# Attention operands in two and a half loads, asked for a pair and two steps ahead, with a second buffer for the turned outputs

## Chip, cores and metric

One core of one Trainium2 chip runs the whole program. The metric is the device time of one execution in microseconds (us): the median of 3 runs before the change is 695.21 us (695.05 to 695.46).

## What is computed

Three layers in a row, in float32. Attention over 2 batches, 8 heads, 768 tokens and a head width of 64, where a query sees only the keys of its own cluster; then a mixing layer over the tokens and a feed-forward layer; then a gated feed-forward layer with a convolution of width 3.

```python
mask = q_assign[:, :, :, None] == k_assign[:, :, None, :]
scores = scale * np.matmul(q, k.transpose(0, 1, 3, 2))
scores = np.where(mask, scores, -1000000000.0)
scores = scores - np.max(scores, axis=-1, keepdims=True)
attn = np.exp(scores)
attn = attn / (np.sum(attn, axis=-1, keepdims=True) + 1e-09)
return np.matmul(attn, v).astype(np.float32)
...
h = xt @ U @ V
u = x + h.transpose(0, 2, 1)
ch = np.maximum(u @ w_ch1, 0.0) @ w_ch2
...
return (h * gate @ w_out).astype(np.float32)
```

`q_assign` and `k_assign` are the indices of the nearest of 16 centroids by cosine.

## The kernel before

**Tiles and steps.** The attention part walks over 96 query tiles of 128 rows: 2 batches, 4 pairs of heads, 2 heads, 6 tiles. One call of `step(n)` handles one tile with work of several tiles in flight: the scores of tile n+2 on TensorE (L342, L353), the exponentials of tile n+1 on ScalarE (L371), the transposes of tile n (L380), the split of tile n-1 into a rounded part (L389, ScalarE) and a rest (L393, VectorE), and one third of the product with the values for an earlier group of three tiles (L404). `s` is the step inside a pair of heads, 0 to 11; the pairs are numbered 0 to 7. The order of instructions on each engine is the order in which the program is written.

**Operands in two parts.** A float32 product is made from rounded (fp32r) parts: high times high, plus high times low, plus low times high. For each head there are two tiles. `cd` (80 partitions) holds the high parts of q and k in its first 64 partitions and one-hot cluster rows in the next 16, so that one matmul gives the high product and the mask. `ab` (128 partitions) holds low parts over high parts, for the two mixed products in one matmul. `load_ops` (L108) fills both by loads on the queue of POOL (GpSimd), which round to fp32r on the way: `ab[0:64]`, `ab[64:128]` and `cd[0:64]`, each 64 rows of q and k (384 KB). `split_ops` (L124) then makes the low parts on POOL, in two subtractions of 64x768: the unrounded q or k (`raw`, loaded through SP by `load_raw`, L89) less the rounded part that the load left in that same place of `ab`.

**Buffers.** Pools `ab` and `cd` have 3 buffers, one per head, so the load of a head reuses what the head three before it left. `raw` has 2, the values `vt` (L120) 2, their unrounded copy `rv` 1.

**Where the preparation stands.** `prep(n)` (L610) prepares the next pair while the present one runs: at s = 0 `load_raw` and the loads of its first head, at s = 2 that head's split, at s = 3 the loads of the values, at s = 4 the loads of the second head, at s = 5 its split, at s = 8 the low part of the values (L633, POOL), at s = 5 or 6 the one-hot rows (L265, SP). The first pair is prepared ahead of the loop (L526 to L532).

**What else is on POOL's queue.** Every third step (s = 1, 4, 7, 10) a group of three tiles ends. `step` then adds 1e-9 to the group's row sums on POOL (L681), and `fin_x` (L423) handles the group before: ScalarE copies the turned outputs out of PSUM into `ats` (L426), VectorE takes the reciprocal of that group's sums (L429), POOL adds the two halves of `ats` (L430) and scales them into `X` in three instructions (L434). `ats` has one buffer: the copy of a group waits until POOL has scaled the group before. ScalarE, VectorE and POOL each work through their queue in order, so a wait at the head of one holds up all behind it.

Of the kernel before, what the change touches and what calls it, by code (L numbers as in the profile page):

```python
# [15 lines left out]
F32 = mybir.dt.float32  # L16
# [8 lines left out]
P = 128  # L25
# [6 lines left out]
def tile_kernel(ctx: ExitStack, tc: tile.TileContext, qk, vv, cen, u_w, v_w, w1, w2, win, wout, conv, out):  # L32
    nc = tc.nc
    B, H, D, _, S = qk.shape
    NC = cen.shape[0] // H
    NP = H // 2
# [31 lines left out]
    a_e = att.enter_context(tc.tile_pool(name="a_e", bufs=3))  # L68
# [16 lines left out]
    raw = {}  # L85
    ops = {}
    vts = {}

    def load_raw(b, p, parts=1):  # L89
        rq, rk = raw[b, p] if (b, p) in raw else take_raw(b, p)  # L90
        h0 = 2 * p
        for i in range(parts):
            c = slice(i * S // parts, (i + 1) * S // parts)
            nc.sync.dma_start(out=rq[:, c], in_=qk[b, h0:h0 + 2, :, 0, c].rearrange("h d s -> (h d) s"))
            nc.sync.dma_start(out=rk[D:2 * D, c], in_=qk[b, h0, :, 1, c])
            nc.sync.dma_start(out=rk[0:D, c], in_=qk[b, h0 + 1, :, 1, c])

    def take_raw(b, p):
        raw[b, p] = tuple(a_raw.tile([P, S], F32, tag=t, name=t) for t in ("rq", "rk"))
        return raw[b, p]  # L100

    def take_ops(b, p, j):
        ab = a_ab.tile([P, 2, S], F32R, tag="ab", name="ab")
        cd = a_ab.tile([80, 2, S], F32R, tag="cd", name="cd")
        ops[b, 2 * p + j] = (ab, cd)
        return ab, cd

    def load_ops(b, p, j):  # L108
        h = 2 * p + j
        ab, cd = take_ops(b, p, j)  # L110
        nc.gpsimd.dma_start(out=ab[0:D], in_=qk[b, h])
        nc.gpsimd.dma_start(out=ab[D:2 * D], in_=qk[b, h])
        nc.gpsimd.dma_start(out=cd[0:D], in_=qk[b, h])

    def load_v(b, p):
        rv = a_v.tile([P, 2, NT, D], F32, tag="rv", name="rv", bufs=1)
        vt = a_v.tile([P, 2, NT, 2 * D], F32R, tag="vt", name="vt")
        nc.sync.dma_start(out=rv, in_=vv[b, p])
        for j in range(2):
            nc.gpsimd.dma_start(out=vt[:, j, :, 0:D], in_=vv[b, p, :, j])  # L120
        vts[b, p] = vt
        return rv, vt

    def split_ops(b, p, j, eng):  # L124
        rq, rk = raw[b, p]
        ab, _ = ops[b, 2 * p + j]
        q0, k0 = (0, D) if j == 0 else (D, 0)
        for r, i, p0 in ((rq, 0, q0), (rk, 1, k0)):
            eng.tensor_sub(ab[p0:p0 + D, i], r[p0:p0 + D], ab[p0:p0 + D, i])


    cent = acon.tile([P, 1, D], F32, name="cent")
# [60 lines left out]
    def split_first(half, which):  # L193
        c = slice(half * HS, (half + 1) * HS)
        if which == "k":
            nc.scalar.copy(cd0[0:D, 1, c], rk0[D:2 * D, c])
            nc.scalar.copy(ab0[0:D, 1, c], rk0[D:2 * D, c])
            nc.gpsimd.tensor_copy(ab0[D:2 * D, 1, c], rk0[D:2 * D, c])
            nc.vector.tensor_sub(ab0[D:2 * D, 1, c], rk0[D:2 * D, c], ab0[D:2 * D, 1, c])
        else:  # L200
            nc.scalar.copy(cd0[0:D, 0, c], rq0[0:D, c])
            nc.scalar.copy(ab0[D:2 * D, 0, c], rq0[0:D, c])
            nc.gpsimd.tensor_sub(ab0[0:D, 0, c], rq0[0:D, c], cd0[0:D, 0, c])
# [7 lines left out]
    def sims(b, p, tiles=range(NT)):  # L211
        rq, rk = raw[b, p]
        if (b, p) not in ohst:
            ohst[b, p] = {"pm": ps_t.tile([P, NT * 4, NC], F32, tag="t", name="sim")}
        pm = ohst[b, p]["pm"]
        for t in tiles:
            for i, (r, cb) in enumerate(((rq, cbq), (rk, cbk))):
                nc.tensor.matmul(
                    pm[:, 4 * t + 2 * i:4 * t + 2 * i + 2, :].rearrange("p g c -> p (g c)"),
                    r[:, t * P:(t + 1) * P], cb[:, p], start=True, stop=True,  # L220
                )

    def sims_onehot(b, p, part):

        v = ohst[b, p]
        if part == 0:
            v["mx"] = a_oh.tile([P, NT * 4, 1], F32, tag="mx", name="mx")
            v["eq"] = a_oh.tile([P, NT * 4, NC], BF16, tag="eq", name="eq")
            v["m2"] = a_oh.tile([P, NT * 4, 1], BF16, tag="m2", name="m2")
            v["oh"] = a_oh.tile([P, NT * 4, NC], BF16, tag="oh", name="oh")  # L230
        onehot_part(v, v["pm"], slice(0, NT * 4), part)
# [15 lines left out]
    def onehot_t(b, p):  # L247
        oh = ohst[b, p]["oh"]
        pt = ps_t.tile([4 * NC, S], BF16, tag="t", name="oht")
        for t in range(NT):  # L250
            nc.tensor.transpose(pt[:, t * P:(t + 1) * P], oh[:, 4 * t:4 * t + 4].rearrange("p g c -> p (g c)"), identb)
        ohst[b, p]["pt"] = pt

    def onehot_rows(b, p):
        pt = ohst.pop((b, p))["pt"]
        os_ = a_oh.tile([4 * NC, S], F32R, tag="os", name="os")
        nc.scalar.activation(os_, pt, AF.Identity, scale=ohs[:, 0:1], bias=ohs[:, 1:2])
        put_rows(b, p, os_, range(2))

    def put_rows(b, p, os_, heads):  # L260
        for j in heads:
            cd = ops[b, 2 * p + j][1]
            for i in range(2):
                r0 = (2 * i + j) * NC
                nc.sync.dma_start(out=cd[D:D + NC, i].bitcast(F32), in_=os_[r0:r0 + NC].bitcast(F32))  # L265
# [65 lines left out]
    def head_of(n):  # L331
        b, r = divmod(n, H * NT)
        h, t = divmod(r, NT)
        return b, h, t
# [87 lines left out]

    def fin_x(g):  # L423
        b, h, t0 = head_of(3 * g)
        at = a_e.tile([P, 3, 2, D], F32, tag="ats", name="ats", bufs=1)
        nc.scalar.copy(at, st.pop(("at", g)))  # L426
        sm = st.pop(("sum", g))
        rs = a_s.tile([P, 3, 1], F32, tag="rs", name="rs")
        nc.vector.reciprocal(rs[:, :, 0], sm)  # L429
        nc.gpsimd.tensor_add(at[:, :, 0], at[:, :, 0], at[:, :, 1])  # L430
        if h == 0 and t0 == 0:
            X[b] = xp.tile([P, NT, DM], F32, tag="x", name="x")
        for i in range(3):
            nc.gpsimd.tensor_tensor(  # L434
                out=X[b][:, t0 + i, h * D:(h + 1) * D], in0=at[:, i, 0],
                in1=rs[:, i].to_broadcast([P, D]), op=ALU.mult,
            )
# [48 lines left out]
    def pump(plan):  # L486

        for j in list(fly):
            j["at"] += 1
            if j["at"] in j["plan"]:  # L490
                j["plan"][j["at"]](j)
            if j["at"] == max(j["plan"]):
                fly.remove(j)
        if plan is THIN:
            free = not fly
        else:
            free = not fly or (fly[-1]["at"] > 1 and fly[-1]["plan"] is FLOW)
        if jobs and free:
            j = jobs.pop(0)
            j["at"], j["plan"] = 0, plan  # L500
            job_dma(j)
            fly.append(j)
# [21 lines left out]


    load_ops(0, 0, 1)  # L526
    rv0 = load_v(0, 0)
    first_pair()
    split_first(1, "q")
    sims(0, 1, range(2))  # L530
    split_ops(0, 0, 1, nc.gpsimd)
    nc.gpsimd.tensor_sub(rv0[1][:, :, :, D:2 * D], rv0[0], rv0[1][:, :, :, 0:D])  # L532

# [76 lines left out]
    def prep(n):  # L610

        pair, s = divmod(n, 2 * NT)
        nxt = pair + 1
        if nxt < B * NP:
            b, p = divmod(nxt, NP)
            for part, at in enumerate((2, 2, 3, 4, 5) if nxt > 1 else (0, 0, 1, 2, 3)):
                if s == at and (nxt > 1 or part > 1):
                    sims_onehot(b, p, part)
            if s == 0:
                if nxt > 1:  # L620
                    load_raw(b, p)
                load_ops(b, p, 0)
            elif s == 2:
                split_ops(b, p, 0, nc.gpsimd)
            elif s == 3:
                st["rv"] = load_v(b, p)
            elif s == 4:
                load_ops(b, p, 1)
            elif s == 5:
                split_ops(b, p, 1, nc.gpsimd)  # L630
            elif s == 8:
                rv, vt = st.pop("rv")
                nc.gpsimd.tensor_sub(vt[:, :, :, D:2 * D], rv, vt[:, :, :, 0:D])  # L633
            if s == (6 if nxt > 1 else 5):
                onehot_t(b, p)
                onehot_rows(b, p)
        if n == NQ - 7:
            queue_chunk(1, lambda: wpc)
        if n >= NQ - 7:
            pump(FLOW)  # L640
        elif n % 2 == 0 and n > 0:
            pump(THIN)

    def step(n):
# [39 lines left out]
        if 0 <= g - 1 < NHALF and r == 0:  # L684
            fin_x(g - 1)
# [194 lines left out]
    for i in range(len(order) + 2):  # L880
# [7 lines left out]
        if 0 <= i - 2:  # L888
            b, f = order[i - 2]
# [57 lines left out]
```

## Time and profile before

| what | value |
|---|---|
| median of 3 runs | 695.21 us |
| profiled execution | 694.12 us, span 692.2 us |
| TensorE (PE) busy | 666.3 us, 96% of the span |
| VectorE (DVE) busy | 445.8 us, 64% |
| ScalarE (ACT) busy | 373.0 us, 54% |
| GpSimd (POOL) busy | 298.9 us, 43% |
| DMA | 61.58 MB, mean 89 GB/s |
| granted TensorE clock, mean | 0.992 |

The span runs from the first to the last instruction of the profiled execution, and that execution's own time is 1.9 us longer. All profile times below are microseconds from the span's start. The attention part lasts to about 290 us. A busy share is a mean over stages, so it doesn't say by itself what a change in one stage is worth; the waits of that stage do.

### The profile page before, as it was taken

The page shows a single profiled execution, that of the slowest core. Times are in us where ns is not written, and L with a number is a line of the kernel's source. Part 1 is how long each engine was busy: PE and PEld are TensorE (multiplying, and loading weights), DVE is VectorE, ACT ScalarE, POOL GpSimd, SP SyncE. Part 2 cuts the span into 40 slices and gives each one's busy share as a digit, 9 for nine tenths or more (in the row PEclk, how much of TensorE's full clock was granted, in tenths as well). Part 3 has the DMA queues.
Part 4 walks back from the last instruction along what each step waited for, and adds up shares of the span by engine and source line. Part 5 has one row for each costly group of instructions (what it writes and reads, how often), then busy time and mean ns, then how long its engine had stood idle before and what let it go on. Part 6 is the DMA issues. An engine that isn't in the chain of part 4 may idle for free.

```text
span 692.2 us, 10474 instructions
## 1 busy us (share of the span) xinstructions
PE 666.3 (96%) x3782; PEld 586.0 (85%) x3782; DVE 445.8 (64%) x833; ACT 373.0 (54%) x750; POOL 298.9 (43%) x392
## 2 busy tenths in 40 slices
PE   8949999999999999999999999999999999999997
PEld 6849999999898998888888888888887788888886
DVE  6837888797978798749831778775237645643400
ACT  6837888787777898424311333433133457653611
POOL 6647666676666642515621333332015634332300
PEclk9988999999999999999999999999999999999999
DMA  9895768685666610301210333442003000000111
GB/s 195 151 136 115 165 116 197 108 192 103 167 119 153 131 35 5 118 31 63 92 62 1 121 123 121 142 133 92 1 30 125 28 0 1 1 32 16 43 49 46
DMA packets 32131, 61.58 MB, mean 89 GB/s; under 512 B 15856, under 2 KB 19568, under 8 KB 32080
## 3 DMA queue, kind: packets, MB, share of 16 engines
q1 hardware_dynamic: 15936, 40.08, 19.6%
q0 software_dynamic: 16144, 20.84, 17.6%
q8 instruction: 30, 0.49, 0.3%
q14 instruction: 21, 0.17, 0.1%
HBM read 56.29 MB, written 3.15 MB: 86 GB/s over the span
## 4 chain that ended last, share of the span: by engine, by line
PE 78%; DVE 8%; issue 3%; DMA 3%; ACT 3%; POOL 2%; ACTq 0%; POOLq 0%; DVEq 0%
PE g L836 10%; PE tr L380 7%; PE pv L404 7%; PE h L713 5%; PE h L715 5%; PE h L714 5%; PE a L730 5%; PE a L729 5%; PE a L731 5%; PE sc L342 3%; PE sc L353 3%; PE po L870 3%; PE po L871 3%; PE po L872 3%; DMA ab<-in_qk_dram 3%
## 5 line engine op out<-in xcount | busy, mean ns | idle before, releaser
L518 POOL TENSOR_TENSOR wl<-wx,wh 128x512 fp32r<-128x512 f32 x48 | 63.0, 1314 | 114.8 <-ACT wh L517 114.5
L393 DVE TENSOR_TENSOR pl<-tr,ph 128x384 fp32r<-128x384 f32 x192 | 97.6, 549 | 21.5 <-ACT ph L389 20.3
L380 PE MATMUL tr<-identf,e 128*128 128x128 f32 x576 | 83.7, 278 | 16.5 <-ACT ats L426 11.4
L389 ACT CAST ph<-tr 128x384 fp32r<-128x384 f32 x192 | 83.5, 485 | 21.3 <-PE tr L380 20.5
L359 DVE TENSOR_SCALAR_CACHE_REDUCE e<-sc 128x768 f32<-128x768 f32 x96 | 90.8, 947 | 0.6 <-PE sc L353 0.6
L718 ACT ACTIVATE rh<-h 128x512 fp32r<-128x512 f32 (+1 forms) x52 | 29.3, 563 | 111.7 <-PE h L715 111.7
L371 ACT ACTIVATE e<-sc,nb 128x768 f32<-128x768 f32 x96 | 88.4, 921 | 1.0 <-DVE e L359 0.9
L380 PEld LDWEIGHTS tr<-identf,e 128*128 128x128 f32 x576 | 66.9, 142 | 25.9 <-ACT ats L426 12.6
L719 DVE SCALAR_TENSOR_TENSOR rl<-h,rh 128x512 fp32r<-128x512 f32 (+1 forms) x52 | 33.7, 648 | 82.9 <-ACT rh L718 82.8
L713 PE MATMUL h<-uh,wh 128*128 128x512 f32 (+1 forms) x208 | 78.1, 376 | 1.6 <-DVE rl L719 1.6
L729 PE MATMUL a<-rh,wh 128*128 128x512 f32 (+1 forms) x208 | 78.1, 376 | 0.5 <-DVE xa L745 0.5
L730 PE MATMUL a<-rl,wh 128*128 128x512 f32 (+1 forms) x208 | 77.8, 374 | 0.5 <-DVE rl L719 0.3
L731 PE MATMUL a<-rh,wl 128*128 128x512 f32 (+1 forms) x208 | 77.6, 373 | 0.0
L715 PE MATMUL h<-uh,wl 128*128 128x512 f32 (+1 forms) x208 | 77.6, 373 | 0.0
L714 PE MATMUL h<-ul,wh 128*128 128x512 f32 (+1 forms) x208 | 77.6, 373 | 0.0
L404 PE MATMUL pv<-ph,vt 128*128 128x384 f32 x192 | 66.0, 344 | 0.2 <-ACT asb L413 0.2
L404 PE MATMUL pv<-pl,vt 128*128 128x384 f32 x192 | 65.3, 340 | 0.0
L517 ACT CAST wh<-wx 128x512 fp32r<-128x512 f32 x48 | 29.8, 620 | 58.3 <-DVE wx L471 58.1
L342 PE MATMUL sc<-ab 128*128 128x384 f32 x192 | 57.4, 381 | 0.7 <-ACT e L371 0.4
L853 POOL TENSOR_TENSOR h<-h,cv 128x768 f32<-128x768 f32 x16 | 29.6, 1850 | 64.5 <-ACT cv L852 64.5
L467 DVE SCALAR_TENSOR_TENSOR wx<-wb,wx 128x512 int32<-128x512 int32 (+3 forms) x52 | 48.3, 928 | 11.4 <-ACT wb L458 9.4
L353 PE MATMUL sc<-cd 80*128 80x384 f32 x192 | 49.7, 341 | 0.0
(136 smaller groups left out, 1493.4 us busy)
## 6 DMA issues: line engine op xcount, KB each, us to landing
raw<-in_w_dram SPq DMA_DIRECT2D x32, 512.0 KB, 3.7
ab<-in_qk_dram POOLq DMA_DIRECT2D x30, 384.0 KB, 5.2
cd<-in_qk_dram POOLq DMA_DIRECT2D x15, 384.0 KB, 6.8
raw<-in_win_dram SPq DMA_DIRECT2D x8, 512.0 KB, 3.7
raw<-in_wout_dram SPq DMA_DIRECT2D x8, 512.0 KB, 3.7
rv<-in_vv_dram SPq DMA_DIRECT2D x8, 384.0 KB, 3.4
vt<-in_vv_dram POOLq DMA_DIRECT2D x16, 192.0 KB, 3.6
out_dram<-o SPq DMA_DIRECT2D x24, 128.0 KB, 1.8
```

The lines of the kernel that those rows point to most:

```text
L359: nc.vector.tensor_scalar(out=e, in0=ps[:, :, 0:HS], scalar1=-SCALE, scalar2=3e38, op0=ALU.mult, op1=ALU.min, accum_out=nb,)
L371: nc.scalar.activation(e, ps[:, :, 0:HS], AF.Exp, scale=SCALE, bias=nb, accum_out=st["sum", n // 3][:, n % 3:n % 3 + 1])
L380: nc.tensor.transpose(pt[:, k, :], e[:, i, k * P:(k + 1) * P], identf)
L389: nc.scalar.copy(st["pt", n // 3][0][:, i * NK:(i + 1) * NK, n % 3, :], st["t", n, i])
L393: nc.vector.tensor_sub(lo, st.pop(("t", n, i)), hi)
L404: nc.tensor.matmul(acc, vt[:, h % 2, k, :], m[:, k].rearrange("p a b -> p (a b)"), start=(k == 0 and i == 0), stop=(k == NT - 1 and i == 1),)
L713: nc.tensor.matmul(ph, wh[:, k, ws], uh[g][:, k, ts], start=(k == 0), stop=False)
L714: nc.tensor.matmul(ph, wh[:, k, ws], ul[g][:, k, ts], start=False, stop=False)
L715: nc.tensor.matmul(ph, wl[:, k, ws], uh[g][:, k, ts], start=False, stop=(k == ND - 1))
L729: nc.tensor.matmul(accs[d][:, 0:n], wh[:, i, ds_], rh, start=(f == 0), stop=False)
L730: nc.tensor.matmul(accs[d][:, 0:n], wh[:, i, ds_], rl, start=False, stop=False)
L731: nc.tensor.matmul(accs[d][:, 0:n], wl[:, i, ds_], rh, start=False, stop=(f == NH - 1))
```

## The change

Each head's operands are loaded as `cd[0:64]` (q and k, 384 KB), `ab[64:128]` (q and k, 384 KB) and only the half of `ab[0:64]` that is used as it lands (192 KB). The other half of `ab[0:64]` is computed from `raw` and the rounded values in `cd`, which are the same numbers. In time, the loads of a pair's first head (and `load_raw`) are asked for at s = 10, two steps before the pair ahead of it begins; the first split follows at s = 1, the second head's loads at s = 3, the values' loads at s = 4, the second split at s = 7. For pair 1 the first head's loads stand in the code ahead of the loop. `ats` gets a second buffer.

```diff
@@ load_ops
-        nc.gpsimd.dma_start(out=ab[0:D], in_=qk[b, h])
+        nc.gpsimd.dma_start(out=cd[0:D], in_=qk[b, h])
         nc.gpsimd.dma_start(out=ab[D:2 * D], in_=qk[b, h])
-        nc.gpsimd.dma_start(out=cd[0:D], in_=qk[b, h])
+        nc.gpsimd.dma_start(out=ab[0:D, 1 - j], in_=qk[b, h, :, 1 - j])
@@ split_ops
-        rq, rk = raw[b, p]
-        ab, _ = ops[b, 2 * p + j]
-        q0, k0 = (0, D) if j == 0 else (D, 0)
-        for r, i, p0 in ((rq, 0, q0), (rk, 1, k0)):
-            eng.tensor_sub(ab[p0:p0 + D, i], r[p0:p0 + D], ab[p0:p0 + D, i])
+
+        ab, cd = ops[b, 2 * p + j]
+        lo, hi = raw[b, p][j], raw[b, p][1 - j]
+        eng.tensor_sub(ab[0:D, j], lo[0:D], cd[0:D, j])
+        eng.tensor_sub(ab[D:2 * D, 1 - j], hi[D:2 * D], ab[D:2 * D, 1 - j])
@@ fin_x
-        at = a_e.tile([P, 3, 2, D], F32, tag="ats", name="ats", bufs=1)
+        at = a_e.tile([P, 3, 2, D], F32, tag="ats", name="ats", bufs=2)
@@ ahead of the loop
     split_first(1, "q")
+    load_ops(0, 1, 0)
     sims(0, 1, range(2))
@@ prep
-            if s == 0:
-                if nxt > 1:
-                    load_raw(b, p)
-                load_ops(b, p, 0)
-            elif s == 2:
+            if s == 1:
                 split_ops(b, p, 0, nc.gpsimd)
             elif s == 3:
+                load_ops(b, p, 1)
+            elif s == 4:
                 st["rv"] = load_v(b, p)
-            elif s == 4:
-                load_ops(b, p, 1)
-            elif s == 5:
+            elif s == 7:
                 split_ops(b, p, 1, nc.gpsimd)
@@ prep, after the one-hot rows
+        if s == 10 and pair + 2 < B * NP:
+            load_raw(*divmod(pair + 2, NP))
+            load_ops(*divmod(pair + 2, NP), 0)
```

The instructions of TensorE, VectorE, ScalarE and SP keep their order; POOL's change. First place: POOL's queue around the start of pair 0, before. `ab_209` and `vt_215` are pair 0's second head and values, `ab_338` with `cd_339` is pair 1's first head.

```order
L120 DMA vt_215<-in_vv_dram 128x6x64 x2
L203 TENSOR_TENSOR ab_196<-rq_111,cd_197 64x384
L129 TENSOR_TENSOR ab_209<-rq_111,ab_209 64x768
L129 TENSOR_TENSOR ab_209<-rk_112,ab_209 64x768
L532 TENSOR_TENSOR vt_215<-rv_214,vt_215 128x12x64
L111 DMA ab_338<-in_qk_dram 64x1536
L112 DMA ab_338<-in_qk_dram 64x1536
L113 DMA cd_339<-in_qk_dram 64x1536
```

The same place now, where pair 1's first head is `ab_282` with `cd_283`.

```order
L120 DMA vt_215<-in_vv_dram 128x6x64 x2
L203 TENSOR_TENSOR ab_196<-rq_111,cd_197 64x384
L111 DMA cd_283<-in_qk_dram 64x1536
L112 DMA ab_282<-in_qk_dram 64x1536
L113 DMA ab_282<-in_qk_dram 64x768
L128 TENSOR_TENSOR ab_209<-rk_112,cd_210 64x768
L129 TENSOR_TENSOR ab_209<-rq_111,ab_209 64x768
L533 TENSOR_TENSOR vt_215<-rv_214,vt_215 128x12x64
```

Pair 1's first loads now stand ahead of the two splits of pair 0 and ahead of its values.

Second place: POOL's queue over the later steps of pair 0, before. `ab_450` with `cd_451` is pair 1's second head, `vt_417` its values; `sum_384` and `sum_476` are the row sums of the second and third group, `ats_558` and `x_563` belong to the first.

```order
L111 DMA ab_450<-in_qk_dram 64x1536
L112 DMA ab_450<-in_qk_dram 64x1536
L113 DMA cd_451<-in_qk_dram 64x1536
L129 TENSOR_TENSOR ab_450<-rq_180,ab_450 64x768
L129 TENSOR_TENSOR ab_450<-rk_181,ab_450 64x768
L681 TENSOR_SCALAR sum_384<-sum_384 128x3
L430 TENSOR_TENSOR ats_558<-ats_558 128x3x64
L434 TENSOR_TENSOR x_563<-ats_558,rs_560 128x64 x3
L633 TENSOR_TENSOR vt_417<-rv_416,vt_417 128x12x64
L681 TENSOR_SCALAR sum_476<-sum_476 128x3
```

The same place now: the second head is `ab_416` with `cd_417`, the values are `vt_451`, the first and second groups' sums are `sum_307` and `sum_386`, the first group's outputs `ats_556` and `x_561`.

```order
L111 DMA cd_417<-in_qk_dram 64x1536
L112 DMA ab_416<-in_qk_dram 64x1536
L113 DMA ab_416<-in_qk_dram 64x768
L681 TENSOR_SCALAR sum_307<-sum_307 128x3
L120 DMA vt_451<-in_vv_dram 128x6x64 x2
L681 TENSOR_SCALAR sum_386<-sum_386 128x3
L430 TENSOR_TENSOR ats_556<-ats_556 128x3x64
L434 TENSOR_TENSOR x_561<-ats_556,rs_558 128x64 x3
L128 TENSOR_TENSOR ab_416<-rk_181,cd_417 64x768
L129 TENSOR_TENSOR ab_416<-rq_180,ab_416 64x768
L630 TENSOR_TENSOR vt_451<-rv_450,vt_451 128x12x64
L681 TENSOR_SCALAR sum_476<-sum_476 128x3
```

Between the second head's loads and its split there is now the whole end of the first group, the second group's sums and the issue of the values' loads; before, the split followed its loads directly.

## Rows read from the trace of the kernel before

**Rows 1.** Page: busy us of each engine; PE's busy tenths in 40 slices

```profile
PE 666.3 (96%) x3782; PEld 586.0 (85%) x3782; DVE 445.8 (64%) x833; ACT 373.0 (54%) x750; POOL 298.9 (43%) x392
...
PE   8949999999999999999999999999999999999997
```

**Rows 2.** Waits, 15 to 275 us, all engines: us in total, times, longest

```profile
POOL ab L129 <- DMA ab<-in_qk_dram: 36.3, 8, 9.1
...
ACT ats L426 <- POOL x L434: 11.1, 1, 11.1
PE tr L380 <- ACT ats L426: 10.7, 3, 9.4
...
DVE rs L429 <- POOL sum L681: 9.2, 2, 8.9
...
ACT ats L426 <- POOL sum L681: 0.5, 2, 0.3
...
ACT ats L426 <- POOL vt L633: 0.3, 1, 0.3
```

**Rows 3.** Timeline of POOL, 14 to 60 us: start, us, instruction [idle before]

```profile
14.73 0.99 POOL L203 TENSOR_TENSOR ab<-rq,cd 64x384 fp32r<-64x384 f32 x1 [3.87 <-ACT cd L201]
...
19.98 2.00 POOL L532 TENSOR_TENSOR vt<-rv,vt 128x768 fp32r<-128x768 f32 x1 [0.21 <-POOL ab L129]
21.93 0.57 POOL L111 DMA_DIRECT2D ab<-in_qk_dram  x1
...
30.48 1.83 POOL L129 TENSOR_TENSOR ab<-rk,ab 64x768 fp32r<-64x768 f32 x1
...
34.34 0.57 POOL L111 DMA_DIRECT2D ab<-in_qk_dram  x1
...
45.09 1.80 POOL L129 TENSOR_TENSOR ab<-rq,ab 64x768 fp32r<-64x768 f32 x1 [9.11 <-DMA ab<-in_qk_dram]
...
48.85 0.22 POOL L681 TENSOR_SCALAR sum<-sum 128x3 f32<-128x3 f32 x1
...
49.82 0.79 POOL L434 TENSOR_TENSOR x<-ats,rs 128x64 f32<-128x64 f32 x3
```

**Rows 4.** Chain that ended last, 20 to 56 us: start, us, what

```profile
21.93 8.28 DMA ab<-in_qk_dram x2
...
34.91 10.04 DMA ab<-in_qk_dram
```

**Rows 5.** Timeline of PE, 35 to 57 us

```profile
35.10 0.82 PE L380 MATMUL tr<-identf,e 128*128 128x128 f32 x6
...
37.73 0.59 PE L342 MATMUL sc<-ab 128*128 128x384 f32 x2
...
41.45 0.34 PE L404 MATMUL pv<-pl,vt 128*128 128x384 f32 x1
51.18 1.88 PE L380 MATMUL tr<-identf,e 128*128 128x128 f32 x6 [9.39 <-ACT ats L426]
...
56.33 0.59 PE L342 MATMUL sc<-ab 128*128 128x384 f32 x2
```

**Rows 6.** Stretches: length, busy of PE, PEld, DVE, ACT, POOL, PEclk, DMA share, GB/s

```profile
51.18:56.33 5.15, 5.08 (x20) 4.41 (x21) 4.07 (x9) 3.82 (x10) 4.63 (x10) 0.54 0.38 118
35.10:37.73 2.63, 2.63 (x22) 2.59 (x20) 2.63 (x7) 2.37 (x7) 0.88 (x2) 1.00 1.75 234
```

**Rows 7.** Timeline of DVE, 37 to 60 us

```profile
49.20 0.76 DVE L467 SCALAR_TENSOR_TENSOR wx<-wb,wx 128x192 int32<-128x192 int32 x1
...
55.40 0.35 DVE L471 SCALAR_TENSOR_TENSOR wx<-wb,wx 128x192 int32<-128x192 int32 x1
...
58.61 0.17 DVE L429 RECIPROCAL rs<-sum 128x3 f32<-128x3 f32 x1
```

**Rows 8.** Timeline of PE's weight loads, 23 to 25 us

```profile
24.00 0.19 PEld L404 LDWEIGHTS pv<-ph,vt 128*128 128x128 f32 x1
```

**Rows 9.** The loads of L113 (the last of a head's three), whole span

```profile
DMA to landing us min/median/max: 6.4/6.8/11.5
```

## Prediction

> **What bounds the kernel now.** I read the page first. TensorE is busy for 666.3 of 692.2 us, and its tenths are at 9 nearly everywhere but for one slice at 4, the third, 35 to 52 us [rows 1]. So the time is TensorE's work plus its holes, and an edit to loads and buffers can only be worth holes. Of the largest hole I asked the waits, all engines together: TensorE's transposes waited once for 9.4 us on ScalarE's copy into `ats`, that copy waited once for 11.1 us on POOL's scaling into X, VectorE's reciprocal waited 8.9 us on POOL's sum, and POOL waited 9.1 us for a load of `ab` [rows 2]. The timeline of POOL orders these: the loads of pair 1's second head are issued from 34.34, its split starts at 45.09 after 9.11 us of idling for the load, and the sum (48.85) and the scaling (49.82) stand behind that split in the queue [rows 3]. The chain of waits agrees: the load takes 10.04 us from 34.91, and the one before it 8.28 us from 21.93 [rows 4]. TensorE's timeline shows the end of it: the last matmul of the step starts at 41.45, the next transposes at 51.18 [rows 5].
>
> POOL waits for a load in 8 places, 36.3 us in all, but only this one reaches TensorE: the others leave ScalarE's copy with 0.5 + 0.3 us of waiting on POOL in the rest of the stretch [rows 2]. At every other split the queue behind it is late by less than the three steps between one group's end and the next.
>
> **What the hole costs.** First, 9.39 us of idle TensorE. Second, what follows it: from the transposes at 51.18 to the scores at 56.33 is 5.15 us, while the same run of instructions three steps earlier, 35.10 to 37.73, takes 2.63 us [rows 5]. The granted clock is 0.54 in the slow stretch and 1.00 in the other [rows 6], so TensorE came back from standing still near the lower of its two levels (1.2 of 2.4 GHz). That is 5.15 - 2.63 = 2.52 us more. Together 11.9 us.
>
> **The change, part by part.**
>
> *Loads earlier, second head.* The split of pair 1's second head moves behind the first group's scaling and the second group's sum. So neither ScalarE's copy of the second group nor VectorE's reciprocal for it stands behind that load any more. This removes the hole by order alone. What is late next is the third group: its sum comes after that split and the values' low part. I follow POOL's queue. The 0.99 us at 14.73 end at 15.72; three issues of 0.57 us at most take it to 17.4; two splits of 1.83 us to 21.1; the values' low part of 2.00 us to about 23.3 [rows 3]. Then the splits of pair 1's first head, whose two loads go out at 15.7 and 16.3: with the 8.28 us of [rows 4] from the first issue they are in by 24.0, and with 11.5 us from the second, the longest of any head's last load [rows 9], by 27.8. That split ends 3.7 us later at 27.7 to 31.5. The second head's loads are issued next, and at 10.04 us [rows 4] from the second issue (28.9) are there by about 38.9; at 11.5 us, after the later start (32.6), by 44.1. Split and values, 3.7 and 2.0 us, bring the third group's sum to 44.7, at worst to 50. VectorE wants it for the reciprocal that now starts at 58.61 [rows 7], and which the removed hole brings to 58.61 - 11.9 = 46.7. By the likelier landing there are 2 us to spare; by the worst one TensorE would lose some 3 us again.
>
> *Loads earlier, first heads.* For pairs 2 to 7 the loads go out one step earlier relative to their split and, on POOL, stand behind the same instructions as before. No split of a first head stopped TensorE before, so this is worth 0.
>
> *Three issues moved ahead at the start.* They push the splits of pair 0's second head and its values back by 3 x 0.57 = 1.7 us. The values' low part ends at 23.3 in place of 21.98, and TensorE first loads its weights from them at 24.00 [rows 8]. Cost 0, with 0.7 us of cover; without that cover the hole would be the overrun itself, at most 1.7 us.
>
> *Half a load less.* 192 KB less for each of 15 heads. Fewer bytes shorten the landing of what is queued behind, not a wait that TensorE sees once the hole is gone. Worth 0; the bound is the 0.8 us that ScalarE's copy still waited on POOL elsewhere.
>
> *The subtraction reads `cd`.* Same shape, same count, 1.83 us each: 0. It waits for the first load in place of a later one, which is in its favour.
>
> *Second buffer for `ats`.* By itself it would not have removed the hole, since VectorE's reciprocal waits 8.9 us on the sum in the same queue and blocks VectorE. With the new order the first group's scaling is done in time with one buffer too. Worth 0 to the same 0.8 us.
>
> *What lay free in the hole.* VectorE did a 0.76 us weight instruction at 49.20 [rows 7] while TensorE stood; now it lies between TensorE's work. In the stretch at full speed VectorE is busy 2.63 of 2.63 us and ScalarE 2.37 [rows 6], so such extras do push. I take 0.4 us of the 0.76, bounds 0 and 1.6 (with the same again for ScalarE).
>
> **Sum.** 9.39 + 2.52 - 0.4 = 11.5 us; 694.12 of the profiled execution becomes 682.6. The median of the runs stands 1.09 us above that execution, which gives 683.7 us. Own bounds: 11.9 + 0.8 gained gives 682.5, 11.9 - 1.6 gives 684.9.
>
> **A rule weighed.** The two VectorE weight instructions have the same shape, 128x192; the one that runs beside POOL's addition takes 0.76 us and the other 0.35 [rows 7]: 0.40 us lost to POOL's neighbourhood. The Trainium skill, "SBUF — State Buffer", section "Who interferes with whom", says that VectorE and GpSimd share one port pair under an exclusive lock, and that a VectorE instruction with two SBUF inputs blocks against a GpSimd instruction that reads SBUF, for the whole of it. With that rule the trace agrees. In this kernel it would mean that a moved split (1.83 us) can hold a VectorE instruction that met a shorter one before, which is the last rival.
>
> **Rivals.**
> 1. *The wait moves to the third group.* The second head's load lands after about 41 us, because the SP loads and the values share the DMA engines. For: the load of 34.91 took 10.04 us [rows 4]. Against: the new one starts 6 us earlier and is 192 KB shorter. Price up to 3.3 us: 683.7 to 687.0.
> 2. *Nothing moves.* The hole has another cause (the copy is late for its own reason), or the same wait returns in full behind the earlier split. Against: four waits of one length in one chain. 695.
> 3. *Slower: each first split waits for its load.* From s = 10 to the split there are three steps, about 8 us; behind the split stand the second head's loads, a sum and a scaling that have three steps of slack again. It decides from a landing of some 15 us; at 17 us each of 6 pairs loses 2 us, plus what rival 1 costs: 683.7 + 12 + 3 = 699. Against: no load took over 11.5 us [rows 9].
> 4. *Slower: VectorE held by moved splits.* Up to 1.83 us for each meeting; seven more meetings than before, all felt by TensorE, give 12.8 us back: 696.5. Against: the number of splits is the same, and only 0.40 us was seen once.
>
> **How the numbers follow.** Forecast 0.79, rival 1 0.10, rival 2 0.05, rival 3 0.03, rival 4 0.03. About 0.2%, 1.4 us, is what a measurement here can tell from no change. Faster by more than that is the forecast and rival 1, 0.89; the same is rival 2, 0.05; slower is rivals 3 and 4, 0.06. The range goes from the lower bound of the forecast, 682.5, to the end of rival 1, 687.0; rivals 2 to 4, 0.11, are left out.
>
> **What would show it.** Right: no wait of `ats` or of a reciprocal on POOL over 1 us, no slice of TensorE at 4, the clock at 1.00 from 20 to 60 us, POOL's splits of pair 1's second head begun before 41 us and POOL's total wait for loads well below 36.3 us. Wrong: a hole of TensorE at 45 to 50 us that ends on a reciprocal (rival 1), the old hole in place (rival 2), POOL waiting 5 us or more at each first split (rival 3), or VectorE's short two-input instructions at 1 to 2 us (rival 4).

## Result: 0.9% faster, a little over half of what was forecast

| what | before | after |
|---|---|---|
| median of 8 runs each, taken together | 695.13 us (692.21 to 696.05) | 688.49 us (686.16 to 691.99) |
| profiled execution | 694.12 us, span 692.2 us | 689.67 us, span 687.8 us |

The ratio is 0.9911, 95% interval 0.9888 to 0.9933. The kernel is 6.6 us faster; the forecast was 683.7 us (11.4 us faster than the 695.13 of this comparison), with a range that ended at 687.0. The sign was right, the size was not. The two profiled executions lie only 4.45 us apart: the one of after is among the longer of its eight.

The page of after, busy us of each engine, then PE's busy tenths and the granted clock in 40 slices:

```profile
PE 668.0 (97%) x3782; PEld 587.1 (85%) x3782; DVE 452.3 (66%) x833; ACT 373.5 (54%) x750; POOL 298.6 (43%) x392
...
PE   8999999998989999999999999999999999999997
...
PEclk9899999999999999999999999999999999999999
```

The slice at 4 of [rows 1] is gone. What is new is VectorE: 452.3 us busy for the same 833 instructions, 6.5 more, and PE has two slices at 8 further on.

The waits of after, 15 to 275 us, all engines (us in total, times, longest):

```profile
PE tr L380 <- DVE pl L393: 8.3, 13, 1.1
...
POOL ats L430 <- DVE rs L429: 7.4, 3, 4.7
...
PE tr L380 <- ACT ats L426: 2.0, 3, 0.7
```

The chain of four waits of [rows 2] has left: no copy into `ats` waits for POOL's scaling, no reciprocal for a sum, and POOL waits for no load at all (36.3 us before). But TensorE's transposes now wait 8.3 us in 13 places for VectorE's rest `pl`; the same row of the kernel before:

```profile
PE tr L380 <- DVE pl L393: 4.5, 8, 0.7
```

POOL's timeline of after, 14 to 52 us, and its part at 68 to 72 us (start, us, instruction [idle before]), which answers to [rows 3]:

```profile
15.88 0.56 POOL L111 DMA_DIRECT2D cd<-in_qk_dram  x1
...
21.33 1.82 POOL L533 TENSOR_TENSOR vt<-rv,vt 128x768 fp32r<-128x768 f32 x1
23.47 1.82 POOL L128 TENSOR_TENSOR ab<-rq,cd 64x768 fp32r<-64x768 f32 x1 [0.31 <-DVE eq L241]
...
27.13 0.54 POOL L111 DMA_DIRECT2D cd<-in_qk_dram  x1
...
36.92 0.59 POOL L430 TENSOR_TENSOR ats<-ats 128x192 f32<-128x192 f32 x1 [5.81 <-ACT ats L426]
...
38.34 1.83 POOL L128 TENSOR_TENSOR ab<-rk,cd 64x768 fp32r<-64x768 f32 x1
...
44.08 0.25 POOL L681 TENSOR_SCALAR sum<-sum 128x3 f32<-128x3 f32 x1
...
50.27 0.59 POOL L430 TENSOR_TENSOR ats<-ats 128x192 f32<-128x192 f32 x1 [2.49 <-DVE rs L429]
...
68.97 1.80 POOL L128 TENSOR_TENSOR ab<-rk,cd 64x768 fp32r<-64x768 f32 x1
70.85 1.83 POOL L129 TENSOR_TENSOR ab<-rq,ab 64x768 fp32r<-64x768 f32 x1
```

The times are close to those that the prediction worked out: second head's loads issued from 27.13 (worked out: 27.7 to 31.5), its split from 38.34 (by about 38.9), the third group's sum at 44.08 (44.7), and POOL waits for that group's reciprocal, not the other way round. For the split and the sum that is luck. The prediction let the split start when its loads land. They landed earlier: the first took 4.2 us from 27.13 and the second 5.4 us from 27.66, so both were in by 33.1. What set 38.34 was the first group's end ahead of it in the queue, for which POOL stood 5.81 us waiting for ScalarE's copy.

The stretches of after (length, busy of PE, PEld, DVE, ACT, POOL, PEclk, DMA share, GB/s) show no hole from 42 to 60 us, where PE is busy all 18 us, and one new thing, a granted clock of 0.50 and 0.65 from 16 to 24 us:

```profile
13.00:16.00 3.00, 3.00 (x26) 2.96 (x25) 2.51 (x5) 2.19 (x5) 1.08 (x2) 0.99 2.46 201
16.00:20.00 4.00, 3.63 (x14) 3.46 (x14) 2.73 (x6) 2.34 (x7) 3.92 (x5) 0.50 1.67 207
20.00:24.00 4.00, 3.51 (x17) 3.13 (x16) 3.79 (x6) 3.11 (x7) 3.61 (x3) 0.65 0.77 148
...
42.00:60.00 18.00, 18.00 (x133) 17.79 (x132) 15.72 (x40) 14.12 (x34) 13.65 (x25) 1.00 0.49 112
```

**Where VectorE's 6.5 us are.** VectorE's groups with shapes kept apart, 15 to 290 us (busy us, mean ns of one | idle before). First before:

```profile
L463 DVE TENSOR_SCALAR wx<-raw 128x512 int32<-128x512 int32 x8 | 6.8, 853 | 0.1
L241 DVE TENSOR_TENSOR eq<-eq,iota 128x384 bf16<-128x384 bf16 x7 | 2.5, 353 | 0.0
L463 DVE TENSOR_SCALAR wx<-raw 96x384 int32<-96x384 int32 x2 | 0.7, 356 | 0.1
L463 DVE TENSOR_SCALAR wx<-raw 128x192 int32<-128x192 int32 x1 | 0.3, 254 | 0.0
```

and after:

```profile
L393 DVE TENSOR_TENSOR pl<-tr,ph 128x384 fp32r<-128x384 f32 x192 | 97.7, 549 | 18.4 <-ACT ph L389 17.5
...
L463 DVE TENSOR_SCALAR wx<-raw 128x512 int32<-128x512 int32 x8 | 9.4, 1174 | 0.1
L241 DVE TENSOR_TENSOR eq<-eq,iota 128x384 bf16<-128x384 bf16 x7 | 3.9, 559 | 0.0
L463 DVE TENSOR_SCALAR wx<-raw 96x384 int32<-96x384 int32 x2 | 2.4, 1190 | 0.1
L463 DVE TENSOR_SCALAR wx<-raw 128x192 int32<-128x192 int32 x1 | 1.2, 1244 | 0.0
```

An instruction is called held below when it takes longer beside an instruction of the other engine than it does elsewhere, and such a pair is called a meeting. L463 is a shift of weight bits (`job_low`, called at s = 8 of a pair), L241 the third of five instructions that make the one-hot rows. Neither was changed or moved, and together they take 16.9 us in place of 10.3. The timeline of VectorE in after shows single ones:

```profile
21.57 1.80 DVE L241 TENSOR_TENSOR eq<-eq,iota 128x384 bf16<-128x384 bf16 x1
...
39.05 1.24 DVE L463 TENSOR_SCALAR wx<-raw 128x192 int32<-128x192 int32 x1
...
70.87 2.02 DVE L463 TENSOR_SCALAR wx<-raw 96x384 int32<-96x384 int32 x1
...
103.69 0.36 DVE L463 TENSOR_SCALAR wx<-raw 96x384 int32<-96x384 int32 x1
```

Lay them against POOL's rows above. L241 begins 0.24 us into the subtraction of 21.33 and ends 0.22 us after it; L463 of 70.87 begins 0.02 us into the split half of 70.85 and ends 0.21 us after it. The same instruction takes 0.36 us at 103.69. TensorE feels it, in its timeline of after:

```profile
72.13 0.49 PE L380 MATMUL tr<-identf,e 128*128 128x128 f32 x3
73.54 0.55 PE L380 MATMUL tr<-identf,e 128*128 128x128 f32 x3 [0.92 <-DVE pl L393]
```

### The profile page after: what moved, and what is told of

The parts are those of the page before. It is cut to its first block, busy times and chain, and to the rows that moved or that the text cites. A ratio compares the mean times of both kernels' runs of the same rounds, so it can differ in the third digit from the quotient of the medians.

```text
span 687.8 us, 10474 instructions
## 1 busy us (share of the span) xinstructions
PE 668.0 (97%) x3782; PEld 587.1 (85%) x3782; DVE 452.3 (66%) x833; ACT 373.5 (54%) x750; POOL 298.6 (43%) x392
## 4 chain that ended last, share of the span: by engine, by line
PE 79%; DVE 9%; issue 4%; ACT 4%; POOL 3%; DMA 1%; ACTq 0%; POOLq 0%; DVEq 0%
PE g L836 10%; PE tr L380 8%; PE pv L404 7%; PE h L713 5%; PE h L714 5%; PE h L715 5%; PE a L730 5%; PE a L729 5%; PE a L731 5%; PE sc L342 4%; PE sc L353 3%; PE po L871 3%; PE po L870 3%; PE po L872 3%; PE sim L218 2%
## 5 line engine op out<-in xcount | busy, mean ns | idle before, releaser
L393 DVE TENSOR_TENSOR pl<-tr,ph 128x384 fp32r<-128x384 f32 x192 | 97.7, 549 | 18.4 <-ACT ph L389 17.5
L430 POOL TENSOR_TENSOR ats<-ats 128x192 f32<-128x192 f32 x32 | 19.7, 616 | 87.6 <-ACT ats L426 80.0
L467 DVE SCALAR_TENSOR_TENSOR wx<-wb,wx 128x512 int32<-128x512 int32 (+3 forms) x52 | 48.4, 931 | 11.4 <-ACT wb L458 9.5
```

The costliest lines, as they stand in the source:

```text
L393: nc.vector.tensor_sub(lo, st.pop(("t", n, i)), hi)
```

## The experiments

The first theory, from these rows: the hole went by order alone and was worth what was forecast; VectorE's L463 and L241, held while POOL subtracts, give back the rest. The rivals: the second buffer or the bytes removed the hole; or the missing gain is the stretch at the lower clock, or only the first pair's. Each ratio is against the kernel before on the same chip: 693.80 us beside the first four kernels, 693.71 beside the next four, 695.07 beside the last four.

**Second buffer alone**, put into the kernel before.

```diff
-        at = a_e.tile([P, 3, 2, D], F32, tag="ats", name="ats", bufs=1)
+        at = a_e.tile([P, 3, 2, D], F32, tag="ats", name="ats", bufs=2)
```

> Before, with the second buffer for ats and nothing else. Theory (the order of POOL's queue makes the hole): the hole of about 9.4 us near 41 to 51 us stays, because VectorE's reciprocal still waits on the sum behind the split; TensorE then ends it on a VectorE or ScalarE row rather than on the copy into ats; time 694 to 696 us, ratio to before 0.999 to 1.001. Rival (the single ats buffer makes the hole): the hole goes and the time falls by 9 us or more.

Measured 693.35 us, ratio 0.9995 (0.9977 to 1.0013). The copy no longer waits, but VectorE does, at the same load. Waits of this kernel, 34 to 60 us:

```profile
POOL ab L129 <- DMA ab<-in_qk_dram: 9.1, 1, 9.1
...
DVE rs L429 <- POOL sum L681: 6.6, 1, 6.6
...
PE tr L380 <- DVE pl L393: 6.0, 1, 6.0
```

The hole is 6.0 us in this profile, where about 9.4 was expected, and from the first L245 to the next L241 it takes 37.45 us in place of 41.60, 4.1 us less. About half of that is lost again ahead of the hole: L241 starts at 21.25 in place of 19.94 after a stretch at a clock of 0.57 (16 to 20 us), and is held for 1.05 us by the values' subtraction. By the medians no gain can be told, and none of more than 1.6 us fits the interval; how much the buffer would gain with the same start stays open.

**The change with one buffer.**

```diff
-        at = a_e.tile([P, 3, 2, D], F32, tag="ats", name="ats", bufs=2)
+        at = a_e.tile([P, 3, 2, D], F32, tag="ats", name="ats", bufs=1)
```

> The change with the one buffer for ats that before has. Theory (order alone removes the hole, the second buffer does nothing): the same as the change, 686 to 690 us, ratio to before 0.989 to 0.994, no wait of the copy into ats on POOL over 1 us. Rival (the second buffer carries part of the gain): slower than the change by 2 us or more, 690 us and up.

Measured 685.76 us, ratio 0.9883 (0.9866 to 0.9900). The hole is gone without the buffer. In its profile no L463 of pairs 1 to 6 is held (0.35 to 0.43 us).

**L463 two steps earlier**, s = 6 instead of 8, in the change.

```diff
-    THIN = {0: job_dma, 2: job_base, 3: job_low, 4: job_high, 5: job_sign, 6: job_put}
+    def job_base_low(j):
+        job_base(j)
+        job_low(j)
+
+    THIN = {0: job_dma, 2: job_base_low, 4: job_high, 5: job_sign, 6: job_put}
```

> The change with VectorE's first weight instruction (L463) moved from step 8 of a pair, where POOL now does the second split and the values' low part, to step 6, where POOL is idle. Theory (what the change gives back is VectorE held by POOL's moved splits): L463 at 128x512 falls from a mean of 1.17 us to about 0.43, the wait of TensorE's transposes on VectorE falls from 8.3 us by 3 us or more, and the time by 3 to 5 us against the change: 683 to 685 us, ratio to before 0.983 to 0.986. Rival (the missing gain is a slow start, a stretch at the lower clock near 16 us that has nothing to do with POOL): L463 is shorter and the time stays within 1 us of the change's 688.5.

Measured 683.48 us (682.78 to 684.44), ratio 0.9857 (0.9842 to 0.9873). VectorE's groups with shapes apart, 15 to 290 us:

```profile
L463 DVE TENSOR_SCALAR wx<-raw 128x512 int32<-128x512 int32 x8 | 6.0, 749 | 0.0
L241 DVE TENSOR_TENSOR eq<-eq,iota 128x384 bf16<-128x384 bf16 x7 | 3.9, 563 | 0.0
L463 DVE TENSOR_SCALAR wx<-raw 96x384 int32<-96x384 int32 x2 | 0.7, 350 | 0.0
```

and TensorE's wait there, 15 to 275 us, near the 4.5 us of before:

```profile
PE tr L380 <- DVE pl L393: 5.0, 9, 0.7
```

L463 is back at its old durations, L241 is not. This profile has the stretch at the lower clock too (0.51 from 16 to 20 us), so that stretch is not what the change was short of. Against the change the ratio is lower by 0.0054, 3.7 us (by 0.0032, 2.2 us, against the second measurement of the change below, where the intervals still overlap). The 5.0 us between the two medians are too many, since the kernel before was 1.3 us faster beside this run.

**The same move in the kernel before**, as a control (same diff).

> Before with the same move of L463 to step 6, as a control. Theory: before has no split beside L463 at step 8, so the time stays within 1.5 us of before, 693.5 to 696. Rival (the move helps whatever POOL does): 3 us or more faster than before.

Measured 693.06 us, ratio 0.9998 (0.9981 to 1.0015). So by itself the move has no gain that can be told, and at most 1.3 us by the interval; what it is worth in the change is mostly a cost of the change taken back. Not all of it need be: in this profile pairs 1 to 5 take 161.28 us, 1.3 less than the 162.59 of before.

**The change again.**

> The change itself once more, beside the others. Theory: 686 to 691 us, spread over several us from run to run, because each meeting of L463 with a split goes one way or the other by tens of ns. Rival (the spread comes from the slow stretch near 16 us alone): in this profile the sum over the pairs 1 to 5 of what they take over 31.6 to 33.9 us is under 1 us.

Measured 687.17 us (685.25 to 688.99), ratio 0.9889 (0.9863 to 0.9915). This profile has the clock at 1.00 from 16 to 24 us, and lasts 2.2 us less in span than the first one of after (685.6); so the lower clock may have cost part of that. But pairs 1 to 5 still take 2.89 us more than before, where the rival wanted less than 1, so the rival that the lower clock explains the whole shortfall falls. Two of its meetings, one that VectorE won and one that it lost, in VectorE's timeline:

```profile
166.76 0.43 DVE L463 TENSOR_SCALAR wx<-raw 128x512 int32<-128x512 int32 x1
...
200.59 2.10 DVE L463 TENSOR_SCALAR wx<-raw 128x512 int32<-128x512 int32 x1
```

and in POOL's:

```profile
166.77 2.12 POOL L129 TENSOR_TENSOR ab<-rq,ab 64x768 fp32r<-64x768 f32 x1
...
200.57 1.83 POOL L129 TENSOR_TENSOR ab<-rq,ab 64x768 fp32r<-64x768 f32 x1
```

In these, whoever is 0.01 to 0.02 us ahead runs at its own duration, and the other is held. In the twelve such pairs of the two profiles of the change (six each, pairs 1 to 6), VectorE was held in five, and each time POOL's start lies 0.01 to 0.02 us ahead; in the other seven VectorE's start is level or ahead, and POOL takes 2.06 to 2.13 us instead of 1.83. The kernel with one buffer lies on the same edge: there VectorE's start is level or up to 0.02 us ahead in all six, so its free L463 is the lucky side. That the spread of the change's runs, 686.16 to 691.99, comes from this is not shown: the kernel before spreads about as widely (692.21 to 696.05 beside the change, 691.27 to 696.64 on the chip of this run).

**Second split at s = 5**, to take POOL away from L463 instead.

```diff
-            elif s == 7:
+            elif s == 5:
                 split_ops(b, p, 1, nc.gpsimd)
```

> The change with the second split at step 5 in place of step 7, so that POOL is done with it before VectorE's L463 at step 8; VectorE's order is untouched. Theory (meetings of L463 with the split give the gain back): L463 at 128x512 under 0.9 us on the mean, 683 to 686 us, ratio to before 0.984 to 0.988. Rival (what counts is where VectorE has its instruction, or the start): as the change, 687 us and up.

Measured 701.34 us, ratio 1.0095 (1.0070 to 1.0120): slower, a miss. L463 is free (0.36, 0.43 us), but the split now meets L245 (`oh` from `eq` and `m`, at s = 5) in each of pairs 1 to 6. One such meeting in this kernel's VectorE timeline:

```profile
59.51 3.26 DVE L245 TENSOR_TENSOR oh<-eq,m 128x384 bf16<-128x384 bf16 x1
```

What POOL did meanwhile, in its timeline:

```profile
58.76 1.75 POOL L120 DMA_DIRECT2D vt<-in_vv_dram  x2
60.52 1.83 POOL L128 TENSOR_TENSOR ab<-rk,cd 64x768 fp32r<-64x768 f32 x1
62.43 2.02 POOL L129 TENSOR_TENSOR ab<-rq,ab 64x768 fp32r<-64x768 f32 x1
```

And TensorE, in its timeline:

```profile
63.29 0.55 PE L380 MATMUL tr<-identf,e 128*128 128x128 f32 x3 [2.15 <-DVE pl L393]
```

L245 takes 3.26 us instead of 0.55, TensorE stands 2.15 us, and pair 1 lasts 33.94 us (L241 to L241, from 55.11 to 89.05) in place of 31.59. The miss speaks for the mechanism: six meetings at 2.35 us, as pair 1 shows, make 14.1 us, and the two medians of this chip lie 14.2 us apart (701.34 and 687.17).

**L241 of the first pair ahead of step 0**, on top of L463 at s = 6.

```diff
-                if s == at and (nxt > 1 or part > 1):
+                if s == at and (nxt > 1 or part > 2):
...
+            sims_onehot(0, 1, 2)
```

> The change with L463 at step 6 and, in pair 0, VectorE's product L241 moved ahead of the first steps, where it no longer meets the low part of the values on POOL near 21.5 us. Theory (that meeting costs pair 0 about 1.4 us): L241 takes 0.35 us, 682 us, 1 to 1.5 us under the kernel with L463 at step 6 alone (683.5). Rival (VectorE's delay there is hidden): 683 to 684 us.

Measured 683.68 us, ratio 0.9841 (0.9816 to 0.9866), level with the kernel without this move: a miss. L241, at 17.29, took 2.27 us, since it met the first split (17.47 to 19.33) instead of the values' subtraction. Here VectorE was 0.18 us ahead and was held all the same.

**The bytes alone**: loads and subtraction of the change, steps and buffer of before.

```diff
-        nc.gpsimd.dma_start(out=ab[0:D], in_=qk[b, h])
+        nc.gpsimd.dma_start(out=cd[0:D], in_=qk[b, h])
         nc.gpsimd.dma_start(out=ab[D:2 * D], in_=qk[b, h])
-        nc.gpsimd.dma_start(out=cd[0:D], in_=qk[b, h])
+        nc.gpsimd.dma_start(out=ab[0:D, 1 - j], in_=qk[b, h, :, 1 - j])
...
-            eng.tensor_sub(ab[p0:p0 + D, i], r[p0:p0 + D], ab[p0:p0 + D, i])
...
+        eng.tensor_sub(ab[0:D, j], lo[0:D], cd[0:D, j])
+        eng.tensor_sub(ab[D:2 * D, 1 - j], hi[D:2 * D], ab[D:2 * D, 1 - j])
```

> Before with the two and a half loads and the subtraction from cd, but the old steps and one buffer for ats. Theory (half a load is worth nothing or little by itself): the hole near 41 to 51 us stays at 8 to 9.5 us, 693 to 695 us, ratio to before 0.997 to 1.000. Rival (bytes on the queues make the hole): a hole under 6 us, 691 us or less.

Measured 696.08 us, ratio 1.0042 (1.0016 to 1.0067): slightly slower. POOL's split starts earlier, since it waits for the first load (`cd`, issued at 33.34) and no longer for the second (`ab[64:128]`, issued at 34.91 before). Its timeline in this kernel:

```profile
40.46 1.83 POOL L128 TENSOR_TENSOR ab<-rk,cd 64x768 fp32r<-64x768 f32 x1 [5.49 <-DMA cd<-in_qk_dram]
```

In [rows 3] the same split starts at 45.09. The hole shortens to 4.3 us, as the rival would have it, but the time does not fall. For with POOL earlier in every pair, the values' subtraction (L633) comes to stand on L463 in each of pairs 1 to 6, 1.80 to 2.05 us each. Waits of this kernel, TensorE, 15 to 290 us:

```profile
PE tr L380 <- DVE pl L393: 11.0, 15, 1.4
PE tr L380 <- ACT ats L426: 6.3, 4, 4.3
```

**The order alone**: steps of the change, three full loads, the old subtraction, one buffer.

```diff
+    load_ops(0, 1, 0)
...
-            if s == 0:
-                if nxt > 1:
-                    load_raw(b, p)
-                load_ops(b, p, 0)
-            elif s == 2:
+            if s == 1:
                 split_ops(b, p, 0, nc.gpsimd)
             elif s == 3:
-                st["rv"] = load_v(b, p)
-            elif s == 4:
                 load_ops(b, p, 1)
-            elif s == 5:
+            elif s == 4:
+                st["rv"] = load_v(b, p)
+            elif s == 7:
                 split_ops(b, p, 1, nc.gpsimd)
...
+        if s == 10 and pair + 2 < B * NP:
+            load_raw(*divmod(pair + 2, NP))
+            load_ops(*divmod(pair + 2, NP), 0)
```

> The change's new steps with before's three full loads, before's subtraction and one buffer for ats. Theory (the new order alone removes the hole): no wait of ats or of a reciprocal on POOL over 1 us in 15 to 275 us, time as the change, 685 to 690 us, ratio to before 0.987 to 0.994. Rival (the half load saved is needed for it): a hole of over 2 us stays near 45 us, 691 us or more.

Measured 684.75 us, ratio 0.9844 (0.9824 to 0.9864). Order alone brings all of the gain, and by its ratio somewhat more than the whole change (0.9889 and 0.9911; the intervals just touch or miss) and than order with the bytes and one buffer (0.9883; the intervals miss). In its profile L463 of pairs 1 to 6 is never held; in pair 1 it starts at 71.40, and POOL's split half at 71.51, 0.11 us behind it (0.11 to 0.13 us in all six pairs, where the change has at most 0.02).

**The bytes alone with L463 at s = 6.**

> Before's steps with the two and a half loads, and VectorE's L463 at step 6. In the same kernel without that move L463 met POOL in every pair (mean 1.49 us at 128x512, 1.97 at 96x384) and the hole was down to 4.3 us. Theory (meetings are what took back the shorter hole): L463 at 0.43 or near, the time falls from 696.1 to 685 to 690 us. Rival (the loads themselves cost it): stays over 693 us.

Measured 690.79 us, ratio 0.9933 (0.9906 to 0.9959), by the ratios 1.1% or some 7.6 us below the bytes alone. L463 is free in every pair, and what is left is the hole, 5.6 us in this profile; the time lies just above what was expected.

**L463 at s = 6 with one buffer.**

> The change with L463 at step 6 and one buffer for ats. Theory (the second buffer is worth nothing once the order is right): 682.5 to 684.5 us, the same as with two buffers (683.5). Rival: over 1 us slower, 684.5 and up.

Measured 683.16 us, ratio 0.9833 (0.9812 to 0.9853). The second buffer is worth nothing here either.

**Pair 1's first loads issued between pair 0's split and its values**, with L463 at s = 6.

```diff
-    load_ops(0, 1, 0)
     sims(0, 1, range(2))
     split_ops(0, 0, 1, nc.gpsimd)
+    load_ops(0, 1, 0)
```

> The change with L463 at step 6 and the loads of pair 1's first head between the two splits of pair 0 and the low part of its values, so that VectorE's L241 finds POOL issuing loads and not reading SBUF. Theory (meetings in pair 0 are part of what is left): L241 of pair 0 under 0.6 us where the start is at full clock, 682 to 683 us, about 1 us under 683.5. Rival (the loads, 3.7 us later, bring a wait of POOL and of VectorE's reciprocal back): 685 us and up.

Measured 682.49 us (682.35 to 685.82), ratio 0.9828 (0.9804 to 0.9853): the lowest median of all, 12.6 us below the kernel before on its chip. VectorE's timeline:

```profile
20.04 0.35 DVE L241 TENSOR_TENSOR eq<-eq,iota 128x384 bf16<-128x384 bf16 x1
...
24.38 1.75 DVE L245 TENSOR_TENSOR oh<-eq,m 128x384 bf16<-128x384 bf16 x1
```

L241 now falls on POOL's issues of loads and is not held; L245 falls on a split and is, by 1.2 us. So the meeting has moved rather than gone: from the first L241 to the next it takes 35.08 us, and 35.36 with the loads as in the change. Against the two kernels with L463 at s = 6 and the loads as in the change the difference is within the intervals.

## Why the prediction was half right

One table holds the account. It goes by the starts of L241 and L245 in VectorE's timeline of each profile; L241 and L245 stand once in every pair at fixed places of the code, and pair 0's L241 comes before the hole, pair 1's behind it.

| profile of | first L241 | to L245 | from there to the next L241 | pairs 1 to 5 |
|---|---|---|---|---|
| before | 19.94 | 4.34 | 41.60 | 162.59 |
| after | 21.57 | 5.79 | 29.83 | 166.95 |
| the change again | 20.04 | 5.35 | 31.10 | 165.48 |
| L463 at s = 6 | 21.58 | 5.82 | 29.54 | 161.74 |
| second split at s = 5 | 20.09 | 5.35 | 29.67 | 175.47 |
| bytes alone | 19.99 | 5.59 | 36.56 | 168.79 |
| order alone | 19.98 | 7.13 | 30.61 | 161.97 |
| loads between | 20.04 | 4.34 | 30.74 | 161.77 |

- **The hole's worth: right.** The prediction had 9.39 + 2.52 = 11.9 us. The stretch with the hole shrinks from 41.60 to 29.67 or 29.54 us where L463 is free in it and L245 takes 0.69 and 0.55 us: 11.9 and 12.1 us.
- **Order, not buffer and not bytes: right.** Order alone and the change with one buffer show it; the buffer alone, and twice one buffer against two, show no gain from the buffer.
- **The third group, and rival 1: right to put it low.** The sum was there at 44.08 and the reciprocal came 6 us later, at 50.01. The way there was wrong, on the safe side: no load set the split's start, and the second load goes out one issue after the first, not two as the working has it (28.9). First splits that wait for loads (rival 3) do not occur.
- **Three issues moved ahead, "cost 0": not so in these profiles, by VectorE.** The cover that was named, TensorE's first use of the values, was enough: in after they are done at 23.15 and first loaded as weights at 27.08. What was not laid beside the later queue was VectorE's L241. In after it is held by the values' subtraction, and L241 to L245 takes 5.79 us in place of 4.34, so 1.45 us; in the second profile it is held by the split ahead of that, 1.01 us. With the loads put between split and values L241 is free and the stretch is back at 4.34, so what POOL does beside it decides; but L245 is held in its place. How much of this is due to the moved issues stays open. In the profile of before L241 is free by 0.04 us only (19.94, the values' subtraction starts at 19.98), and in two other kernels with the old order at the start it is held, 1.05 us (buffer alone) and 1.59 us (bytes alone).
- **"The subtraction reads `cd`" and "Half a load less", both 0: not 0 where they stand alone.** They bring POOL forward, and in the kernel before that puts POOL onto L463 in each of pairs 1 to 6: 0.4% slower. With L463 out of the way the same loads are 0.7% faster than before.
- **The second buffer, 0: right in the sum, with a small loss in one place.** Pair 3 takes 32.03 to 32.07 us in every profile with two buffers and L463 and L245 free, and 31.68 to 31.71 in every one with a single buffer, some 0.35 us less. What makes it so stays open.
- **0.4 us for the VectorE instruction that lay free in the hole: wrong, but small.** L467 took 0.32 us in after instead of the 0.76 of [rows 7], and the stretch gained the full 11.9.
- **The step that failed** is the price of the moved second split for VectorE, which the sum has at nothing. The prediction had the mechanism as rival 4, with a chance of 0.03 and the argument "the number of splits is the same, and only 0.40 us was seen once". What counts is not the number but where they stand. At s = 7 the split falls on L463 at s = 8, their starts within 0.02 us, in each of pairs 1 to 6. In place of nothing, pairs 1 to 5 give back 4.36 us in the one profile of the change and 2.89 us in the other. I had followed POOL's new times against POOL's own queue and the reciprocal, and never against VectorE's other instructions; L463 was read in no row. Without the held L463 the forecast gain is nearly there: 683.7 us is a ratio of 0.9836, and order alone came to 0.9844, the four kernels with the new order and L463 at s = 6 to 0.9828 to 0.9857.

So the profile of after adds up. The hole gives 11.93. The slow start takes 21.57 - 19.94 = 1.63, L241 1.45, and the rest of the first pair is 29.83 - 29.67 = 0.16 longer than with no meeting (L463 at 39.05, held 1.0 us, is hardly felt): 8.69 us gained by the time of pair 1's L241. Pairs 1 to 5 give back 166.95 - 162.59 = 4.36 us: the three pairs in which L463 is held are 1.25, 1.22 and 1.53 us longer than before, and pair 3 is 0.37 longer, which goes with the second buffer and not with L463: it is as long with L463 at s = 6. That leaves 4.33; the spans differ by 4.4. For the second profile of the change it is 11.93 - 0.10 - 1.01 - 1.43 = 9.39 in the first pair (the 1.43 with L245, held 1.24 us at 25.39), less 2.89 in pairs 1 to 5, 6.5; the spans differ by 6.6. Rival 4 had seven meetings at 1.83 us; there were two or three in pairs 1 to 5, at some 1.25 to 1.5 us of TensorE's time each. With meetings in all of pairs 1 to 5, as in the bytes alone, those pairs give back 168.79 - 162.59 = 6.2 us.

The prediction also took the wrong kind of instruction. It looked for VectorE's short instructions with two SBUF inputs. L463 reads one tile from SBUF and is held as fully, 2.02 us for 0.36. Of this the Trainium skill, "SBUF — State Buffer", section "Who interferes with whom", says that `tensor_scalar` is among the operations that can enter a mode which takes both port pairs, when its operands allow it, and that whoever issues first has the shared pair for its whole instruction. No run here shows which mode L463 is in. With the second statement the trace agrees in the twelve pairs of starts, where the loser waits out the other's instruction; L241 at 17.29, recorded 0.18 us ahead and held, does not fit it by the recorded starts. L393, which reads one input from PSUM, kept its mean of 549 to 550 ns in every run.

## What to carry to other kernels

When an engine's long instruction is moved, lay its new time against every instruction of the engine it can hold, not only against its own queue: here 0.36 to 0.43 us of VectorE beside 1.83 us of POOL took back up to 1.5 us of TensorE in a pair. Where two starts lie 0.02 us apart, either engine can be the one that is held; 0.11 us apart was enough in the one profile of order alone, and moving the short instruction by two steps was worth more than the buffer and the bytes, which gave nothing. Price a hole as idle time plus the slow return: that sum, 11.9 us, held to 0.2 us.

## What the runs showed of the hardware beyond that

- L245 in the kernel with the second split at s = 5 is recorded from 59.51, when POOL was still issuing loads (58.76 to 60.51), yet ended only at 62.77, after the whole split half of 60.52 to 62.35. It needs 0.55 us, and there was 1.0 us before the subtraction began. In after the same instruction at 61.60 lay wholly beside such issues (60.84 to 62.60) and took 0.55 us. L241 at 17.29, above, is a second case: it needs 0.35 us, and the subtraction is recorded 0.18 us behind it, after an issue of a load. Why the hold comes ahead of the subtraction's recorded start stays open.
- In order alone, L241 took 3.13 us from 19.98: it began inside one POOL subtraction (19.32 to 21.13) and ended after the next (21.10 to 22.89). A held instruction does not always get the gap between two.
- The granted clock near the lower of its two levels (0.50, 1.2 of 2.4 GHz) from 16 to 20 us came and went between profiles of the same kernel: in after and not in the change again. TensorE was busy 3.00 of 3.00 us from 13 to 16 us, just before it fell; in the kernel with the loads between it was busy 3.00 of 3.00 us too, and the clock stayed at 1.00. What sets it stays open; L241 starts 1.6 us later with it.
